# Attention's steps put in another order, a float64 decode of four operations, and 48 warm-up products more

## The chip, the cores and the metric

One Trainium2 chip, one of its cores. The metric is device time in microseconds (us) of one execution, from the first to the last instruction with what lies around them. The kernel before takes 933.77 us (median of 3 runs, 930.19 to 936.92). Engines: PE multiplies matrices, DVE and ACT work elementwise, POOL does a little elementwise work and the gathers, SP issues most of the transfers. Each engine runs its own instructions strictly in the order of the program and waits where the next one's input isn't there or its output tile isn't free.

## The reference

Three stages, one behind the other, on 2304 tokens (4 batches of 576) of width 512 (8 heads of 64):

- attention by landmarks: for every batch and head, 32 landmark queries and keys are means over 18 tokens; three softmax score matrices A (576x32), Bm (32x32), C (32x576); six Newton steps turn Bm into an approximate inverse Z; the result is A Z C v.
- a dense layer: `h = x @ w_in` (512 to 2048), `softplus(h) @ w_out` (2048 to 512).
- a mixture of experts: argmax over 8 gates picks one expert per token, `relu(x @ w1[e]) @ w2[e]`, scaled by two gate factors.

`w_in` and `w_out` arrive as float64 (the factors of 8 and of 1/sqrt make them so), q, k, v as float32. A float64 weight is read as two 32-bit words and turned into a float32 on the chip ("decode"); every float32 operand of the dense layers is then split into a high and a low fp32r part, and each product is made of three (high x high, high x low, low x high).

## The kernel before, in words

**Attention** works on 8 groups of four heads (group g: batch g // 2, heads 4 (g % 2) on). Its work is cut into named steps: K (load k and q of a group), V (load v), T (24 transposes of k and q on PE, evicted by ACT, L180 to L192), M (landmarks), A and C (scores and softmax, most of the DVE work), E (transposes of C's exponentials and the product with v), N (Bm and the Newton steps, for a batch), F (the last products, `ps_x`, evicted into `xo`, of which there are three, and stored to `xT_d` in DRAM, L363 to L387), W (one of 16 blocks of 128 columns of `w_in`: loaded, decoded, split into `whi`, `wlo`, L389), O (the same for the first block of `w_out`), X (the first 256 tokens' x, loaded back from DRAM and split, L414). `PLAN` (L38) lists these steps, and the place in that list is a step's priority. The order on each engine is then worked out by a planner with modelled costs: an instruction that is ready by its estimate goes ahead of one with a higher priority that isn't. So a step late in the list can run early if its tiles are free. In attention the order of the list is thus a wish; from the dense layer on (`with tc.manual_schedule()`, L848) each engine's order is that of the program text.

Loads of k, q and v have three tiles each (`ld`, L147), so K3 waits for K0's tiles. W, O and X have two tiles `raw` of their own in the same pool. Small matrix products of a constant tile `dense` with itself (`warm`, L161) are put ahead of real work on PE into the tile that the work will overwrite; they keep PE busy and compute nothing that is used: 18 at the start, one per tensor in T (at `h == 0`), and some in A, C, E and F.

**Decode** (L87): ACT takes the absolute value of the upper word (L93), DVE shifts it left by 3 and masks it (L94), puts the sign in (L96), puts three bits of the lower word in (L98), and multiplies by 0 where the magnitude is under a bound (L101, the guard). A yield stands after each DVE operation, so that the caller can spread them.

**Dense layer.** Chunks of 256 tokens. The first three chunks (`JOINT`) take turns over 8 pairs of blocks; 24 turns in all. Per turn i: 24 products of `gemm1`, softplus (ACT: abs L636, exp L637, +1 L638, ln L640; DVE: L641, then a turn later L647, L648; ACT copies the high part, L654; DVE the low part, L655), and 12 products of `gemm2` for turn i - 2. Beside these turns the 21 blocks of weights not yet there are decoded ("jobs", `weights()`, L580), one per turn: `units(n)` runs the next n pieces of the job list, `U` says how many at three places of a turn (behind L647 and L648 of turn i - 1 and `gemm1`; behind softplus; ahead of `gemm2`). The tiles `t`, `u`, `l`, `d` of softplus have one buffer each. The first three jobs are done ahead of the first turn (`units(15)`, five pieces each).

Pools opened later lie over memory of closed ones. Most wait tile by tile (`reuse_waits="tile"`); `gp` (L451), which lies lowest and holds among others the tiles `wg`, `tri_b`, `one_b`, doesn't: its instructions wait for whole pools below it. Before, that is `ld`, opened first (L147) and so lowest. The first instructions of the dense part are two loads of x, a load of a weight block, the two loads of `wg` on SP, and the casts to `tri_b` and `one_b` on DVE (L850 to L855).

The pieces of a job are, with the line of each operation:

```
piece 1: L93 (ACT), L94 (DVE)      piece 2: L96      piece 3: L98
piece 4: L101, next load           piece 5: L109 (ACT), L110 (DVE)
```

Of the kernel before, what the change touches and what calls it, by code (L numbers as in the profile page):

```python
# [10 lines left out]
F32 = DT.float32  # L11
# [24 lines left out]
HALF = S // 2  # L36
NB = 1
PLAN = """  # L38
M0 M1 K2 T0 V0 C0 A0 M2 T1 E0 A1 V1 C1 T2 K3 C2 M3 K4 K5 T3 E1 V2 K6 M4 T4 V3 W0 W1 C3 A2 N0 F0 T5 N1 A3 V4 A4 W2 E2
V5 M5 W3 E3 K7 M6 C4 C5 T6 C6 E4 A5 N2 M7 W4 V6 F1 V7 T7 N3 C7 E5 E6 A6 A7 E7 O0 F2 W5 W6 X0 F3 W7 W8 W9  # L40
"""
NWA = 10
JOINT = 3
# [1 line left out]
TAIL = 0, 2, 1, 0, 1, 1, 0, 0, 1, 0, 1, 0, 0, 0, 1, 1  # L45
NBASE = NTILE + NE // 2 + 1
LEAD = 1
U = 1, 2, 2
LAG = 2


# [32 lines left out]
CONST, COFF = const_table()  # L84


def decode_f64(nc, pool, src, shape, tag="dect", guard="vector", **kw):  # L87

    w = src.rearrange("p a (n two) -> p a n two", two=2)
    lo32, hi32 = w[:, :, :, 0], w[:, :, :, 1]  # L90
    t = pool.tile(shape, I32, tag=tag, name="dect", **kw)
    a = pool.tile(shape, F32, tag="deca", name="deca", **kw)
    nc.scalar.activation(a, hi32.bitcast(F32), AF.Abs)  # L93
    nc.vector.tensor_scalar(t, a.bitcast(I32), 3, 0x3FFFFFFF, ALU.logical_shift_left, ALU.bitwise_and)  # L94
    yield
    nc.vector.scalar_tensor_tensor(t, hi32, -0x40000000, t, ALU.bitwise_and, ALU.bitwise_or)  # L96
    yield
    nc.vector.scalar_tensor_tensor(t, lo32, 29, t, ALU.logical_shift_right, ALU.bitwise_or)  # L98
    yield
    if guard == "vector":  # L100
        nc.vector.scalar_tensor_tensor(a, a, 3.4332275390625e-05, t.bitcast(F32), ALU.is_ge, ALU.mult)  # L101
    else:
        nc.gpsimd.tensor_scalar(a, a, 3.4332275390625e-05, None, ALU.is_ge)
        nc.gpsimd.tensor_tensor(a, a, t.bitcast(F32), ALU.mult)
    yield a


# [11 lines left out]
def moe_nystrom_kernel(ctx: ExitStack, tc: tile.TileContext, q, k, v, w_in, w_out, w_gate, w_ogate, w1, w2,  # L119
# [24 lines left out]


    with ExitStack() as actx:
        ld = actx.enter_context(tc.tile_pool(name="a_ld", bufs=3))  # L147
        a1 = actx.enter_context(tc.tile_pool(name="a1", bufs=1))
        a2 = actx.enter_context(tc.tile_pool(name="a2", bufs=2))
        a3 = actx.enter_context(tc.tile_pool(name="a3", bufs=3))  # L150
        pt = actx.enter_context(tc.tile_pool(name="pt", bufs=2, space=PSUM))
        pss = actx.enter_context(tc.tile_pool(name="pss", bufs=2, space=PSUM))
        psm = actx.enter_context(tc.tile_pool(name="psm", bufs=1, space=PSUM))
# [7 lines left out]
        def warm(ps):  # L161

            nc.tensor.matmul(ps, dense[:, :128], dense, start=True, stop=True)
# [16 lines left out]
        def transposes(r, g):  # L180
            for nm in ("k", "q"):
                xt = a2.tile([128, 4, HALF], F32, tag=nm + "T", name=nm + "T", bufs=3)
                for h in range(4):
                    ps = pt.tile([128, 512], F32, tag="pt", name="ps_t")
                    if h == 0:
                        warm(ps)
                    for c in range(3):
                        nc.tensor.transpose(ps[:, c * TP:(c + 1) * TP], r[nm][:, h, c * 128:(c + 1) * 128],
                                            ident[:TP, :TP])
                    nc.scalar.activation(xt[:, h], ps[:, :HALF], AF.Copy)  # L190
                    yield
                r[nm + "T"] = xt  # L192
# [195 lines left out]

        def decode_w_in(i):  # L389
            n = FF // 16  # L390
            raw = ld.tile([128, 8 * n], I32, tag="raw", name="raw", bufs=2).rearrange("p (k f) -> p k f", k=4)
            nc.sync.dma_start(raw, w_in.bitcast(I32).rearrange("(k p) f -> p k f", p=128)[:, :, 2 * n * i:2 * n * (i + 1)])
            a = list(decode_f64(nc, a3, raw, [128, 4, n], bufs=2))[-1]
            split_hi_lo(nc, a, whi[0][:, :, i * n:(i + 1) * n], wlo[0][:, :, i * n:(i + 1) * n], nc.gpsimd)
# [8 lines left out]
            return [R[2 * b], R[2 * b + 1]]  # L403

        nc.scalar.preload_act_table_set("natural_log_exp_and_others")
        ps0 = psm.tile([128, 512], F32, tag="sm0", name="ps_0")
        for _ in range(18):
            warm(ps0)
        nc.sync.dma_start(cst[:, :128], consts[:, :128])
        nc.sync.dma_start(lmc, consts[:, CONST.shape[1] - 98:])  # L410
        load_qk(0)
        load_qk(1)
        nc.sync.dma_start(cst[:, 128:], consts[:, 128:CONST.shape[1] - 98])
        def prep_x0():  # L414
            xr = ld.tile([128, 4, CH], F32, tag="raw", name="x0r", bufs=2)
            nc.sync.dma_start(xr, xT_d[0].rearrange("(k p) n -> p k n", p=128)[:, :, :CH])
            split_hi_lo(nc, xr, x0[0], x0[1], nc.gpsimd)

        def prep_wo0():
            raw = ld.tile([128, 2 * DM], I32, tag="raw", name="raw", bufs=2)  # L420
            nc.sync.dma_start(raw, w_out.bitcast(I32)[:128, :])
            a = list(decode_f64(nc, a3, raw.unsqueeze(1), [128, 1, DM], bufs=2))[-1]
            split_hi_lo(nc, a[:, 0], wo0[0], wo0[1], nc.gpsimd)
# [128 lines left out]
    with ExitStack() as mctx:  # L552
# [295 lines left out]
        with tc.manual_schedule():  # L848
# [32 lines left out]
            for j in (1, 2):  # L881
                xs[j] = split_x(xr.pop(0))
                load_w(j)
            units(15)
            for i in range(len(order) + LAG):
                fast[0] = len(order) - np_ <= i - LAG + 1 < len(order)
                if i == len(order):
# [207 lines left out]
```

## Time and profile before

| | |
|---|---|
| median of 3 runs | 933.77 us (930.19 to 936.92) |
| the profiled execution | 929.7 us, its span 927.9 us |
| busy share of the span | PE 93%, PE weight loads 77%, DVE 73%, ACT 63%, POOL 23% |
| attention | until the first `gemm1` product at 159.0 us |
| turns with decode | to about 286 us |

The profile cuts the span into stretches; for each it gives the busy time of each engine, the clock that PE was granted (1.00 is full speed) and how busy the transfers were. The timeline lists instructions in order of time: start, duration, engine, line, and in brackets the idle time of the engine ahead of it with what ended it.

### The profile page before, as it was taken

What the parts mean: (1) busy time and instruction counts of PE and PEld (TensorE: products, weight loads), DVE (VectorE), ACT (ScalarE), POOL (GpSimd) and SP (SyncE); (2) the same over time, 40 slices, a digit from 0 to 9 for tenths busy, and PEclk for the clock granted to TensorE, in tenths of its full rate; (3) what the DMA queues carried; (4) which work ended last, traced back from release to release, by engine and by line L of the source; (5) the groups of instructions that cost most, each with busy time, mean ns of one, the idle gap of its engine ahead of it and who ended that gap; (6) DMA issues with size and microseconds to landing.
All of it is one profiled execution on the core that took longest, in us unless ns stands there. A gap on an engine that the chain in (4) does not pass through costs nothing.

```text
span 927.9 us, 15459 instructions
## 1 busy us (share of the span) xinstructions
PE 867.0 (93%) x5796; PEld 717.6 (77%) x5796; DVE 678.3 (73%) x1153; ACT 586.8 (63%) x958; POOL 212.7 (23%) x109
## 2 busy tenths in 40 slices
PE   7877897889999999999999999998999999999996
PEld 4444564777878899999899998886778888878885
DVE  1796975788886445565556454657899998899994
ACT  2465644666666555555555556464888988988883
POOL 0122200000000000000000000015566676766662
PEclk8899998899999999999999999999999999999998
DMA  9975345222210000100111000141116559531600
GB/s 234 227 207 166 99 146 172 91 91 69 91 46 23 24 1 24 33 15 23 46 47 46 1 24 1 46 183 46 35 46 246 188 169 362 202 129 35 222 31 32
DMA packets 49661, 90.93 MB, mean 98 GB/s; under 512 B 5487, under 2 KB 32239, under 8 KB 47536
## 3 DMA queue, kind: packets, MB, share of 16 engines
q1 hardware_dynamic: 41552, 74.43, 25.5%
q0 software_dynamic: 3680, 10.78, 3.6%
q10 hardware_dynamic: 4352, 4.72, 1.5%
q8 instruction: 46, 0.75, 0.3%
q14 instruction: 31, 0.25, 0.1%
HBM read 134.46 MB, written 15.48 MB: 162 GB/s over the span
## 4 chain that ended last, share of the span: by engine, by line
PE 54%; DVE 20%; DMA 9%; ACT 9%; issue 6%; SPq 1%; POOL 1%; ACTq 0%; DVEq 0%; POOLq 0%
PE ps_h L626 16%; PE acc L665 13%; PE ps_g L964 8%; PE ps_y L990 7%; DMA raw<-in_moe_w 3%; DMA raw<-in_moe_w_in 3%; DVE lo L486 3%; DVE dect L98 2%; DVE dect L96 2%; ACT hi L484 2%; DVE gl L655 2%; PE ps_lg L690 2%; ACT gh L654 2%; DVE l L648 1%; DVE d L647 1%
## 5 line engine op out<-in xcount | busy, mean ns | idle before, releaser
L486 DVE TENSOR_TENSOR lo<-raw,hi 128x1024 fp32r<-128x1024 f32 x129 | 223.4, 1758 | 14.5 <-ACT hi L484 14.2
L484 ACT ACTIVATE hi<-raw 128x1024 fp32r<-128x1024 f32 x176 | 177.2, 1063 | 12.1 <-DMA raw<-in_moe_w 11.1
L626 PE MATMUL ps_h<-xh,whi 128*128 128x256 f32 x512 | 148.1, 289 | 7.9 <-DVE d L647 6.1
L493 POOL DMA_INDIRECT xg<-x_d,gidx x23 | 37.8, 1645 | 497.3 <-ACT t L636 486.3
L626 PE MATMUL ps_h<-xl,whi 128*128 128x256 f32 x512 | 145.6, 284 | 0.3 <-DVE xl L110 0.3
L626 PE MATMUL ps_h<-xh,wlo 128*128 128x256 f32 x512 | 145.5, 284 | 0.0
L655 DVE TENSOR_TENSOR gl<-l,gh 128x512 fp32r<-128x512 f32 x72 | 49.8, 692 | 122.0 <-ACT gh L654 120.5
L486 POOL TENSOR_TENSOR lo<-raw,hi 128x1024 fp32r<-128x1024 f32 x47 | 118.4, 2522 | 38.8 <-ACT hi L484 38.7
L626 PEld LDWEIGHTS ps_h<-xh,whi 128*128 128x128 f32 x512 | 98.5, 192 | 13.5 <-DVE d L647 9.9
L626 PEld LDWEIGHTS ps_h<-xl,whi 128*128 128x128 f32 x512 | 98.7, 193 | 1.9 <-DVE xl L110 0.5
L626 PEld LDWEIGHTS ps_h<-xh,wlo 128*128 128x128 f32 x512 | 98.7, 193 | 0.0
L665 PE MATMUL acc<-woh,gh 128*128 128x512 f32 x240 | 96.0, 400 | 0.0
L665 PE MATMUL acc<-wol,gh 128*128 128x512 f32 x240 | 94.3, 393 | 0.0
L665 PE MATMUL acc<-woh,gl 128*128 128x512 f32 x240 | 94.0, 392 | 0.0
L636 ACT ACTIVATE t<-ps_h 128x512 f32<-128x512 f32 x72 | 42.6, 591 | 70.4 <-PE ps_h L626 49.2
L640 ACT ACTIVATE l<-t 128x512 f32<-128x512 f32 x72 | 45.5, 632 | 55.1 <-DVE gl L655 55.1
L990 PE MATMUL ps_y<-hi,hh 128*128 128x512 f32 x184 | 76.0, 413 | 0.3 <-ACT hh L982 0.2
L990 PE MATMUL ps_y<-hi,hlo 128*128 128x512 f32 x184 | 73.1, 397 | 1.7 <-DVE hlo L983 1.6
L964 PE MATMUL ps_g<-hi,x0l 128*128 128x512 f32 x184 | 73.7, 400 | 0.4
L990 PE MATMUL ps_y<-lo,hh 128*128 128x512 f32 x184 | 72.2, 392 | 0.0
L964 PE MATMUL ps_g<-lo,x0h 128*128 128x512 f32 x184 | 72.1, 392 | 0.0
L964 PE MATMUL ps_g<-hi,x0h 128*128 128x512 f32 x184 | 72.0, 392 | 0.0
(265 smaller groups left out, 1804.1 us busy)
## 6 DMA issues: line engine op xcount, KB each, us to landing
raw<-in_moe_w SPq DMA_DIRECT2D x88, 1024.0 KB
raw<-in_moe_w_in SPq DMA_DIRECT2D x16, 512.0 KB
raw<-in_moe_w_out SPq DMA_DIRECT2D x16, 512.0 KB
x_d<-x SPq DMA_DIRECT2D x9, 514.0 KB
k<-in_k SPq DMA_DIRECT2D x8, 576.0 KB
q<-in_q SPq DMA_DIRECT2D x8, 576.0 KB
v<-in_v SPq DMA_DIRECT2D x8, 576.0 KB
xT_d<-xo ACTq DMA_DIRECT2D x16, 288.0 KB
```

Of the source, the lines that this page charges most:

```text
L96: nc.vector.scalar_tensor_tensor(t, hi32, -0x40000000, t, ALU.bitwise_and, ALU.bitwise_or)
L98: nc.vector.scalar_tensor_tensor(t, lo32, 29, t, ALU.logical_shift_right, ALU.bitwise_or)
L484: nc.scalar.activation(w[0][:, us], raw[i][:, us], AF.Copy)
L486: eng.tensor_tensor(w[1][:, us], raw[i][:, us], w[0][:, us].bitcast(F32), ALU.subtract)
L493: nc.gpsimd.indirect_dma_start(out=xg, out_offset=None, in_=src, in_offset=bass.IndirectOffsetOnAxis(ap=gidx[:, s:s + 1], axis=0))
L626: nc.tensor.matmul(ps[:, i], a[:, kk], b_[:, kk], start=n == 0, stop=n == 11)
L636: nc.scalar.activation(t, h, AF.Abs)
L640: nc.scalar.activation(l, t, AF.Ln, bias=1.0)
L655: nc.vector.tensor_tensor(gl, l, gh.bitcast(F32), ALU.subtract)
L665: nc.tensor.matmul(acc[tt], a[:, i, ts_], b_[f], start=f == 0 and n == 0, stop=f == NFF - 1 and n == 2)
L964: nc.tensor.matmul(ps, a[:, kk], b_[:, kk], start=n == 0, stop=n == 11)
L990: nc.tensor.matmul(y, a[:, kk], b_[:, kk], start=half == 0 and n == 0, stop=half == 1 and n == 11)
```

## The change

Three things at once. **Decode**: L93 scales by 2^-112 while it takes the absolute value, so that the mask and the guard are left out; the last operation writes the result. A job has four pieces instead of five: `units(15)` becomes `units(12)` and `U` goes from 1, 2, 2 to 1, 1, 2. **Attention**: another `PLAN`, in which blocks of `w_in` come late (W0 to W7 in the last third, W8 and W9 at the end); the blocks, O and X take their tiles from those of k, q and v in turn instead of from two of their own; `ld` is opened last, so that `a1` (with `dense`) and `a2` lie lowest; K1's load stands in `PLAN`, the constants but `lmc` come in one load behind K0's. **Warm-up products**: none of the 18 at the start; four per tensor in T instead of one.

```diff
 PLAN = """
-M0 M1 K2 T0 V0 C0 A0 M2 T1 E0 A1 V1 C1 T2 K3 C2 M3 K4 K5 T3 E1 V2 K6 M4 T4 V3 W0 W1 C3 A2 N0 F0 T5 N1 A3 V4 A4 W2 E2
-V5 M5 W3 E3 K7 M6 C4 C5 T6 C6 E4 A5 N2 M7 W4 V6 F1 V7 T7 N3 C7 E5 E6 A6 A7 E7 O0 F2 W5 W6 X0 F3 W7 W8 W9
+K1 T0 M0 M1 A0 C0 T1 K2 M2 C1 K3 V0 A1 K4 V1 T2 E0 C2 E1 T3 M3 N0 V2 K5 K6 V3 T4 A2 C3 A3 F0 V4 E2 M4 A4 M5 T5 K7 E3
+N1 X0 V5 M6 C4 T6 C5 C6 E4 M7 V6 V7 N2 A5 E5 W0 F1 N3 W1 W2 E6 W3 T7 A6 W4 O0 C7 A7 W5 F2 W6 E7 W7 F3 W8 W9
 """
-U = 1, 2, 2
+U = 1, 1, 2
...
-    nc.scalar.activation(a, hi32.bitcast(F32), AF.Abs)
-    nc.vector.tensor_scalar(t, a.bitcast(I32), 3, 0x3FFFFFFF, ALU.logical_shift_left, ALU.bitwise_and)
+    nc.scalar.activation(a, hi32.bitcast(F32), AF.Abs, scale=2.0 ** -112)
+    nc.vector.tensor_scalar(t, a.bitcast(I32), 3, None, ALU.logical_shift_left)
     yield
-    nc.vector.scalar_tensor_tensor(t, hi32, -0x40000000, t, ALU.bitwise_and, ALU.bitwise_or)
+    nc.vector.scalar_tensor_tensor(t, hi32, -0x80000000, t, ALU.bitwise_and, ALU.bitwise_or)
     yield
-    nc.vector.scalar_tensor_tensor(t, lo32, 29, t, ALU.logical_shift_right, ALU.bitwise_or)
-    yield
-    if guard == "vector":
-        nc.vector.scalar_tensor_tensor(a, a, 3.4332275390625e-05, t.bitcast(F32), ALU.is_ge, ALU.mult)
-    else:
...
+    nc.vector.scalar_tensor_tensor(a.bitcast(I32), lo32, 29, t, ALU.logical_shift_right, ALU.bitwise_or)
     yield a
...
-        ld = actx.enter_context(tc.tile_pool(name="a_ld", bufs=3))
         a1 = actx.enter_context(tc.tile_pool(name="a1", bufs=1))
         a2 = actx.enter_context(tc.tile_pool(name="a2", bufs=2))
         a3 = actx.enter_context(tc.tile_pool(name="a3", bufs=3))
+        ld = actx.enter_context(tc.tile_pool(name="a_ld", bufs=3))
...
                     ps = pt.tile([128, 512], F32, tag="pt", name="ps_t")
-                    if h == 0:
-                        warm(ps)
+                    warm(ps)
...
         def decode_w_in(i):
-            raw = ld.tile([128, 8 * n], I32, tag="raw", name="raw", bufs=2).rearrange("p (k f) -> p k f", k=4)
+            raw = ld.tile([128, NC6 * 4 * D], I32, tag="kqv"[i % 3], name="raw")
+            raw = raw[:, :8 * n].rearrange("p (k f) -> p k f", k=4)
...
-        ps0 = psm.tile([128, 512], F32, tag="sm0", name="ps_0")
-        for _ in range(18):
-            warm(ps0)
-        nc.sync.dma_start(cst[:, :128], consts[:, :128])
         nc.sync.dma_start(lmc, consts[:, CONST.shape[1] - 98:])
         load_qk(0)
-        load_qk(1)
-        nc.sync.dma_start(cst[:, 128:], consts[:, 128:CONST.shape[1] - 98])
+        nc.sync.dma_start(cst, consts[:, :CONST.shape[1] - 98])
         def prep_x0():
-            xr = ld.tile([128, 4, CH], F32, tag="raw", name="x0r", bufs=2)
+            xr = ld.tile([128, 4, CH], F32, tag="k", name="x0r")
...
-            raw = ld.tile([128, 2 * DM], I32, tag="raw", name="raw", bufs=2)
+            raw = ld.tile([128, 2 * DM], I32, tag="q", name="raw")
...
-            units(15)
+            units(12)
```

## Rows read from the trace of the kernel before

**Rows 1.** Busy us per stretch: PE, PEld, DVE, ACT, POOL, PEclk, DMA share, GB/s.
```profile
9.00:60.00 51.00, 41.00 (x471) 26.22 (x464) 31.73 (x79) 23.21 (x57) 5.20 (x4) 0.80 0.91 225
60.00:75.00 15.00, 11.17 (x165) 7.35 (x164) 15.00 (x36) 10.34 (x27) 4.89 (x3) 1.00 0.73 206
100.00:145.00 45.00, 42.54 (x636) 28.83 (x633) 39.57 (x121) 23.50 (x55) 3.82 (x3) 1.00 0.34 100
145.00:159.00 14.00, 8.44 (x39) 3.27 (x38) 5.51 (x9) 7.12 (x12) 0.00 (x0) 0.84 0.81 261
178.00:286.00 108.00, 98.69 (x604) 84.45 (x604) 94.45 (x152) 68.29 (x118) 0.00 (x0) 1.00 0.23 71
```

**Rows 2.** The guard, L101, alone: DVE busy per stretch, with its count.
```profile
0.00:80.00 80.00, 6.54 (x8) 0.87 0.85 217
80.00:145.00 65.00, 2.03 (x3) 0.97 0.40 118
```

**Rows 3.** Waits from 0 to 160 us: total us, times, longest.
```profile
ACT deca L93 <- DMA raw<-in_moe_w_in: 10.0, 6, 3.8
ACT xo L383 <- DMA xT_d<-xo: 6.0, 4, 2.5
```

**Rows 4.** Timeline of PE, two warm-up products that follow each other.
```profile
137.70 0.38 PE L163 MATMUL ps_x<-dense 128*128 128x512 bf16 x1
137.91 0.38 PE L163 MATMUL ps_et<-dense 128*128 128x512 bf16 x1
```

**Rows 5.** Timeline of DVE, one turn with decode.
```profile
209.31 0.69 DVE L110 TENSOR_TENSOR wol<-deca,woh 128x512 fp32r<-128x512 f32 x1 [0.62 <-ACT woh L109]
...
210.38 0.70 DVE L96 SCALAR_TENSOR_TENSOR dect<-raw,dect 128x512 int32<-128x512 int32 x1
211.11 0.69 DVE L98 SCALAR_TENSOR_TENSOR dect<-raw,dect 128x512 int32<-128x512 int32 x1
...
212.44 0.69 DVE L648 TENSOR_TENSOR l<-l,d 128x512 f32<-128x512 f32 x1
213.04 0.68 DVE L101 SCALAR_TENSOR_TENSOR deca<-deca,dect 128x512 f32<-128x512 f32 x1
213.83 0.69 DVE L655 TENSOR_TENSOR gl<-l,gh 128x512 fp32r<-128x512 f32 x1
214.44 0.68 DVE L641 SCALAR_TENSOR_TENSOR u<-u,t 128x512 f32<-128x512 f32 x1
```

**Rows 6.** Timeline of ACT, the same turn.
```profile
208.67 0.61 ACT L109 ACTIVATE woh<-deca 128x512 fp32r<-128x512 f32 x1
209.19 0.65 ACT L93 ACTIVATE deca<-raw 128x512 f32<-128x512 f32 x1
209.74 0.58 ACT L636 ACTIVATE t<-ps_h 128x512 f32<-128x512 f32 x1
...
213.16 0.63 ACT L654 ACTIVATE gh<-l 128x512 fp32r<-128x512 f32 x1
...
215.09 0.62 ACT L109 ACTIVATE whi<-deca 128x512 fp32r<-128x512 f32 x1
```

**Rows 7.** Timeline of ACT, a turn after the last job.
```profile
297.64 0.60 ACT L636 ACTIVATE t<-ps_h 128x512 f32<-128x512 f32 x1 [1.78 <-PE ps_h L626]
298.27 0.63 ACT L637 ACTIVATE t<-t 128x512 f32<-128x512 f32 x1
298.94 0.63 ACT L638 ACTIVATE u<-t 128x512 f32<-128x512 f32 x1
299.48 0.61 ACT L654 ACTIVATE gh<-l 128x512 fp32r<-128x512 f32 x1
```

**Rows 8.** Timeline of ACT, the third of the jobs ahead of the turns.
```profile
167.20 0.63 ACT L109 ACTIVATE woh<-deca 128x512 fp32r<-128x512 f32 x1 [2.70 <-DVE deca L101]
```

**Rows 9.** Timeline of DVE, the first cast of the dense part.
```profile
144.02 0.23 DVE L854 CAST tri_b<-cst 128x128 bf16<-128x128 f32 x1 [0.26 <-PE ps_cv L355]
```

**Rows 10.** Timeline of PE, attention's last warm-up product.
```profile
156.16 0.59 PE L163 MATMUL ps_x<-dense 128*128 128x512 bf16 x1 [2.13 <-ACT xo L383]
```

More of the change, by code (lines that the diff above doesn't have):

```diff
@@ L84, with decode_f64 @@
 CONST, COFF = const_table()
-def decode_f64(nc, pool, src, shape, tag="dect", guard="vector", **kw):
+def decode_f64(nc, pool, src, shape, tag="dect", **kw):
     w = src.rearrange("p a (n two) -> p a n two", two=2)
@@ L92, in decode_f64 @@
     a = pool.tile(shape, F32, tag="deca", name="deca", **kw)
-    nc.scalar.activation(a, hi32.bitcast(F32), AF.Abs)
-    nc.vector.tensor_scalar(t, a.bitcast(I32), 3, 0x3FFFFFFF, ALU.logical_shift_left, ALU.bitwise_and)
+    nc.scalar.activation(a, hi32.bitcast(F32), AF.Abs, scale=2.0 ** -112)
+    nc.vector.tensor_scalar(t, a.bitcast(I32), 3, None, ALU.logical_shift_left)
     yield
-    nc.vector.scalar_tensor_tensor(t, hi32, -0x40000000, t, ALU.bitwise_and, ALU.bitwise_or)
+    nc.vector.scalar_tensor_tensor(t, hi32, -0x80000000, t, ALU.bitwise_and, ALU.bitwise_or)
     yield
-    nc.vector.scalar_tensor_tensor(t, lo32, 29, t, ALU.logical_shift_right, ALU.bitwise_or)
-    yield
-    if guard == "vector":
-        nc.vector.scalar_tensor_tensor(a, a, 3.4332275390625e-05, t.bitcast(F32), ALU.is_ge, ALU.mult)
-    else:
-        nc.gpsimd.tensor_scalar(a, a, 3.4332275390625e-05, None, ALU.is_ge)
-        nc.gpsimd.tensor_tensor(a, a, t.bitcast(F32), ALU.mult)
+    nc.vector.scalar_tensor_tensor(a.bitcast(I32), lo32, 29, t, ALU.logical_shift_right, ALU.bitwise_or)
     yield a
```

## The prediction

> **What bounds the kernel now.** I read the busy share by stretch first, since the three stages have different limits, then the waits of attention, then the timelines of DVE and ACT for one turn of the dense layer. Nothing behind the turns with decode is touched: the experts, the later chunks and their tiles stay as they are. So two stretches decide.
>
> In attention no engine is full for long [rows 1]. From 9 to 60 us PE is busy 41 of 51 us at a granted clock of 0.80 (a mean of its two levels, 1.2 and 2.4 GHz) and the transfers run at 0.91; from 60 to 75 us DVE never rests; from 100 to 145 us PE does 42.5 of 45 and DVE 39.6; from 145 to 159 us all of them wait, mostly for the stores of `xo`. ACT loses 10.0 us in six waits for blocks of `w_in` and 6.0 us in four for those stores [rows 3]. Attention is thus PE's in its second half, and a mixture in its first.
>
> In the turns with decode DVE (94 of 108 us) and PE (99) both look nearly full [rows 1], yet neither sets the time. Take one turn from high copy to high copy, 208.67 to 215.09: 6.42 us [rows 6]. Follow who waits for whom [rows 5, 6]: L109 on ACT, 0.64 later L110 on DVE, then L94 and at 210.38 L96, 0.73 later L98, 1.33 later (past L647) L648, 0.72 later L654 on ACT, 0.67 later L655 on DVE, and 1.26 later (past ACT's L640, which needs the tile `l` that L655 has read) the next L109. These steps sum to 6.42. L101 at 213.04 runs while ACT makes L654: it isn't in that ring.
>
> **The change, part by part.** First the turns, where the order can be followed by hand. The new pieces are: L93, L94; L96; L98; L109 with L110. By i = 2 the job list stands so that one turn holds, on DVE: L647, L648, L94, L655, L641, L96, L98, L110; on ACT: L93, L636, L637, L638, L654, L640, L109. The new ring goes the other way round through ACT: L109 to L93 0.52, L93 to L636 0.55 [rows 6], L636 to L637 0.63, L637 to L638 0.67, L638 to L654 0.54 [rows 7], L654 to L655 0.67, L655 to L641 0.61, L641 to L96 0.61 (as L655 to L641, no dependence), L96 to L98 0.73 [rows 5], L98 to L109 0.73 (as L648 to L654, with the hop). Sum 6.26. The guard's 0.69 us are gone, but they weren't in the old ring, and the new order puts L96 and L98 between softplus and the next high copy, with L93 ahead of the next L636. That is 0.16 less per turn; 108 us hold 17 turns: **-2.7**. Bounds: -12 (17 x 0.69, everything the guard took) to +2 (hops 0.1 dearer than read). I take the ring. PE's own work per turn, 98.7/108 x 6.42 = 5.9, still hides.
>
> Ahead of the turns, three jobs follow one another through ACT and DVE; the third's L109 waited 2.70 us for decode [rows 8]. Two such waits lose 0.69 each: -1.4. Against it stands `gp`. Before, it lies over `ld` and its first cast went at 144.02, just behind the last reader of v, `ps_cv` [rows 9], while F3 was still waiting for stores. With `ld` opened last, `gp` lies over `a1` and `a2`; the last reader there is the warm-up product ahead of F3's last `ps_x`, at 156.16 [rows 10]. DVE then has the casts, four L110 for x at 0.61, and a decode of 1.8 (0.46 + 0.73 + 0.61, from rows 5) still to do, some 5 us, of which 2.8 fit ahead of the first `gemm1` at 159.0: +2.2. SP has the second and third weight block queued behind the `wg` loads that wait likewise; they are needed 3 us later than the first, so at most another 3 us. Net **+1**, bounds -1.4 to +5.
>
> Attention, against its 159.0 us:
> - 48 more warm-up products. Two in a row start 0.21 apart [rows 4]: 10.1 us of PE if none falls in a gap, 0 if all do. PE is busy 80% of 9 to 60 us and 95% of 100 to 145; T also waits for ACT's evictions. I take **+6**.
> - 11 guards, 8.6 us of DVE [rows 2]. They count only where DVE never rests: **-3**, bounds -8.6 to 0.
> - No block of `w_in` can be loaded early: W0 needs K6's tile, W2 that of V5, W8 that of V7, which is free only behind E7. ACT's 10 us of waits at those loads [rows 3] fall away in the first half. PE and DVE had other work or waited for K and V beside them: **-5**, bounds -10 to 0.
> - The same blocks now come in the last third. 8 of 11 decodes lay before 80 us [rows 2]; at 1.8 us each that is 14.4 us of DVE put where it rests 5.4 of 45 us and is rid of three guards (2.0): 7 us too much, up to 14 if its rests can't be used. It frees 20 us of DVE in the first half, where PE has 3.8 idle us beside a full DVE [rows 1]: **+2**, bounds -4 to +14. If those late loads land late, ACT waits in order, and softmax and evictions are queued behind them.
> - F2 stands ahead of E7, no longer next to F3, so the three `xo` tiles meet four stores, not eight: **-3** of the 6.0 [rows 3], bounds -6 to 0.
> - The start: 18 products that ran while nothing was loaded, and the constants behind K0 instead of split; T0 stands first and DVE's softmax may start earlier. The clock of 0.80 would give back at most 8 us of 41 if it rose to full. I take 0, bounds -8 to +2.
>
> L93 with a scale and L94 with one operation are taken at their old length: L637 runs with a scale in 0.63 us against L638's 0.63 with none [rows 7]. Attention: 6 - 3 - 5 + 2 - 3 = **-3**. All: -3 + 1 - 2.7 = -4.7. The profiled execution took 929.7, so 925.0 by it; the median of the runs is 4.1 above that, and the forecast against it is **929**.
>
> **The rivals.**
> *The turns follow DVE's load.* If the ring has slack that I don't see, a turn loses all of the guard's 0.69 us: -11.7 instead of -2.7, 920. For it: DVE is busy 87% of that stretch [rows 1], PE's floor of 5.9 leaves room. Against: L101 starts beside L654 and DVE still idles 0.62 ahead of L110 [rows 5]. The Trainium skill says the same in "VectorE: DVE Perf Modes", section "Rules for kernel authors": for chained operations, keep down their number. By that rule the time would be 920; the trace doesn't bear it out for an operation off the ring. Chance 0.14.
>
> *Attention keeps the gain of its first half.* The loads of k, q, v have the transfers for themselves, ACT's waits go in full (-10 for -5), the start gives 3, and the late blocks fit into rests (-2 for +2): -12 more, 917. For: from 9 to 60 us DVE rests 19 of 51 us and PE 10 [rows 1], with next to nothing but those loads to wait for. Against: PE's second half is full before any product is added. Chance 0.20.
>
> *The late blocks lengthen the end.* DVE has no rest from about 100 us to F3, W5 to W9 are decoded on DVE and ACT ahead of what the dense part needs first, and the first `gemm1` starts after 170 instead of 159.0. Price: 14 instead of 2, and +4 at the start of the turns: 945. It decides if DVE is over 95% busy from 100 us to the end of attention. For: 7 us too much by the sum above. Against: W8 and W9 are needed only in later turns, and 14 us behind 145 us stand half empty. Chance 0.22.
>
> *All added warm-up products lie on PE's path*, and the front gives nothing (+4 and +5): 938. Chance 0.06. *The decode costs as before*, if an absolute value with a scale or a shift without a mask ran slower: 11 and 21 decodes, 0.2 us each, would be under 4 us in the ring; it stays inside the forecast.
>
> **How the numbers follow.** A change of 1%, 9.3 us, is about what can be told from none. The forecast has 0.38, its own range 922 to 939. Faster by over 1% (under 924.4): the first two rivals, 0.34. Within: forecast and warm-up case, 0.44. Slower (over 943.1): 0.22. The range leaves out the outer halves of the second and third rivals: 913 to 947.
>
> **What would show it.** Turn: L109 to L109 at 6.2 to 6.3 us, L98 straight ahead of L109, no idle of DVE but behind L109 and L654. `tri_b` right behind the last warm-up product. Few waits of ACT for `w_in` before 60 us, and the fourth softmax (A3) before 75 us. DVE over 90% busy in the last 45 us of attention, PE too; the first `gemm1` at 152 to 162. Wrong: a turn under 6.0 or over 6.5, attention's end outside 148 to 168, or any difference behind the turns.

## The result, and the profile after

The changed kernel takes **919.01 us** (median of four runs, 917.9 to 920.92) against 934.41 us for the kernel before on the same chip in the same job (four runs, 930.19 to 936.92): a ratio of 0.9862, interval 0.9834 to 0.9889. The forecast was 929, its own case 922 to 939, the whole range 913 to 947. The time lies in the range, but not in the forecast's own case; it is near rival 2's 917. The profiled execution took 920.92, with a span of 919.1 against 927.9.

PE's granted clock over the span comes first, from the page of the changed kernel (40 slices of 23 us, in tenths of full speed; 9 is 90% or more).

```profile
PEclk9999997799999999999999999999999999999998
```

The first six slices, 138 us, now have 90% or more. The two at 7 are where attention ends and the turns start. Next the busy time by stretch of the changed kernel, with the columns of [rows 1].

```profile
9.00:60.00 51.00, 48.31 (x628) 32.66 (x629) 26.95 (x77) 25.88 (x66) 0.00 (x0) 1.00 0.85 195
60.00:75.00 15.00, 14.97 (x213) 9.16 (x213) 8.80 (x30) 6.96 (x15) 0.00 (x0) 1.00 0.64 169
100.00:145.00 45.00, 39.36 (x467) 23.86 (x465) 37.25 (x91) 27.58 (x58) 9.24 (x7) 0.97 0.55 167
145.00:159.00 14.00, 12.46 (x75) 10.45 (x76) 9.26 (x19) 6.41 (x12) 2.65 (x2) 0.72 0.79 246
```

From 9 to 60 us PE is busy 48.31 us, not 41.00, at 1.00 instead of 0.80. DVE has fallen from 31.73 to 26.95 there, and from 15.00 to 8.80 in the next stretch. What the clock does there is seen best from 20 to 30 us, first in the kernel before, then in the changed one (with its next 10 us).

```profile
20.00:30.00 10.00, 10.00 (x97) 5.42 (x96) 3.97 (x20) 2.96 (x8) 0.00 (x0) 0.58 1.10 258
```
```profile
20.00:30.00 10.00, 9.28 (x145) 5.81 (x140) 8.06 (x26) 5.65 (x15) 0.00 (x0) 1.00 1.11 246
30.00:40.00 10.00, 10.00 (x125) 7.13 (x118) 9.13 (x29) 4.58 (x12) 0.00 (x0) 1.00 0.76 176
```

Before, PE never rested in that stretch, at a granted 0.58, and got through 97 products; the changed kernel does 145 in 9.28 busy us at 1.00, about 10 of them warm-up products (2 before). A busy share alone doesn't show such a loss.

From 100 to 145 us PE and DVE are at 87% and 83%: neither is full, though eight decodes fall into that stretch. The blocks are counted by the last operation of a decode, L101, alone (DVE busy and count), to be set against [rows 2]; DVE is the column behind the length.

```profile
0.00:80.00 80.00, 0.00 (x0) 1.00 0.79 185
80.00:145.00 65.00, 7.67 (x10) 0.98 0.55 166
```

The view of waits from 0 to 160 us of the changed kernel (total, times, longest) answers to [rows 3].

```profile
ACT deca L96 <- DMA raw<-in_moe_w_in: 4.2, 2, 3.0
ACT deca L96 <- DMA raw<-in_moe_w_out: 2.5, 1, 2.5
```

ACT's wait for blocks of `w_in` fell from 10.0 to 4.2 us, and the 6.0 us at the stores of `xo` are gone. The 2.5 us for a block of `w_out` lie behind attention; the kernel before had one such wait, of 1.4 us.

The front can be followed by four marks: the start of each softmax (A0 to A3, the transpose of `asm`), the first and second `wbd` (F0, F1), the first `gemm1`, and the first softplus of the dense part (L628; L636 before).

| us | A0 | A1 | A2 | A3 | F0 | F1 | first `gemm1` | first softplus | turn |
|---|---|---|---|---|---|---|---|---|---|
| before | 30.8 | 41.4 | 59.5 | 84.4 | 76.4 | 119.8 | 159.0 | 167.7 | 6.42 |
| after | 21.4 | 31.6 | 42.7 | 57.9 | 61.1 | 110.4 | 149.7 | 164.4 | 6.22 |

The gain is 9.4 us at A0, 26.5 at A3, 15.3 at F0, 9.4 at F1 and 9.3 at the first `gemm1`. Attention thus wins in its first half and gives part of it back in the last third. Then 6.0 of the 9.3 are lost at once: from the first `gemm1` to the first softplus it is 14.7 us, before 8.7. This is the timeline of the changed kernel there, PE's products first, then DVE, ACT and the DMA queue of SP, and last two rows of ACT in the kernel before.

```profile
147.43 0.61 PE L160 MATMUL ps_x<-dense 128*128 128x512 bf16 x1
149.67 0.58 PE L618 MATMUL ps_h<-x0h,whi 128*128 128x256 f32 x1 [0.37 <-ACT xo L379]
```
```profile
147.21 0.69 DVE L101 SCALAR_TENSOR_TENSOR deca<-raw,dect 128x512 int32<-128x512 int32 x1
148.08 0.23 DVE L846 CAST tri_b<-cst 128x128 bf16<-128x128 f32 x1 [0.18 <-PE ps_x L160]
...
150.73 0.69 DVE L107 TENSOR_TENSOR xl<-xr,xh 128x512 fp32r<-128x512 f32 x1 [0.27 <-ACT xh L106]
```
```profile
147.94 0.63 ACT L106 ACTIVATE whi<-deca 128x512 fp32r<-128x512 f32 x1 [2.31 <-DVE deca L101]
...
152.17 0.68 ACT L96 ACTIVATE deca<-raw 128x512 f32<-128x512 f32 x1
154.90 0.63 ACT L106 ACTIVATE woh<-deca 128x512 fp32r<-128x512 f32 x1 [2.05 <-DVE deca L101]
158.07 0.69 ACT L96 ACTIVATE deca<-raw 128x512 f32<-128x512 f32 x1 [2.54 <-DMA raw<-in_moe_w_out]
...
164.41 0.58 ACT L628 ACTIVATE t<-ps_h 128x512 f32<-128x512 f32 x1
```
```profile
150.48 0.37 SPq L845 DMA_DIRECT2D wg<-in_moe_w_gate  x1
...
151.56 30.79 SPq L567 DMA_DIRECT2D raw<-in_moe_w_out  x8
```
```profile
149.12 0.67 ACT L93 ACTIVATE deca<-raw 128x512 f32<-128x512 f32 x1
...
159.40 0.63 ACT L109 ACTIVATE woh<-deca 128x512 fp32r<-128x512 f32 x1 [0.44 <-ACT xo L383]
```

The 6.0 us come apart into three pieces. Before, ACT began the first weight block at 149.12, long ahead of the first `gemm1` at 159.0, between evictions of `xo`, and made its high copy 0.4 us behind that product. Now ACT is late with it: it makes W9's high copy at 147.94 after 2.31 us of waiting for DVE, then the four of x and two evictions of `xo`, and only then, at 152.17, the first L96; the high copy at 154.90 is 5.2 us behind the first `gemm1`: +4.8. The second weight block lands late and stops ACT 2.54 us at 158.07: +2.5. The two jobs behind the first are shorter than their 3.9 us before: -1.4.

`tri_b` goes 0.04 us behind the end of the last warm-up product (147.43 + 0.61), as predicted, but it delays nothing that can be seen: the first L96 is 2.50 us behind the first `gemm1` here, and 2.50 in run 8, where the casts stand elsewhere. The second weight block is issued behind the `wg` loads, yet these hold it by 0.1 us at most: its tile is that of the second chunk's x, whose split (L107) ends at 151.42, and it goes at 151.56. It then takes 6.5 us to land.

Last, one turn of the changed kernel, ACT from high copy to high copy and DVE beside it. It answers to [rows 5, 6].

```profile
181.99 0.63 ACT L106 ACTIVATE woh<-deca 128x512 fp32r<-128x512 f32 x1 [1.30 <-DVE deca L101]
182.52 0.67 ACT L96 ACTIVATE deca<-raw 128x512 f32<-128x512 f32 x1
183.10 0.57 ACT L628 ACTIVATE t<-ps_h 128x512 f32<-128x512 f32 x1
183.70 0.63 ACT L629 ACTIVATE t<-t 128x512 f32<-128x512 f32 x1
184.37 0.64 ACT L630 ACTIVATE u<-t 128x512 f32<-128x512 f32 x1
184.91 0.61 ACT L646 ACTIVATE gh<-l 128x512 fp32r<-128x512 f32 x1
...
188.21 0.63 ACT L106 ACTIVATE woh<-deca 128x512 fp32r<-128x512 f32 x1 [1.30 <-DVE deca L101]
```
```profile
185.55 0.69 DVE L647 TENSOR_TENSOR gl<-l,gh 128x512 fp32r<-128x512 f32 x1 [0.55 <-ACT gh L646]
186.16 0.68 DVE L633 SCALAR_TENSOR_TENSOR u<-u,t 128x512 f32<-128x512 f32 x1
186.76 0.69 DVE L99 SCALAR_TENSOR_TENSOR dect<-raw,dect 128x512 int32<-128x512 int32 x1
187.48 0.69 DVE L101 SCALAR_TENSOR_TENSOR deca<-raw,dect 128x512 int32<-128x512 int32 x1
188.88 0.69 DVE L107 TENSOR_TENSOR wol<-deca,woh 128x512 fp32r<-128x512 f32 x1 [0.70 <-ACT woh L106]
```

Start to start the ring has 0.53, 0.58, 0.60, 0.67, 0.54, 0.64, 0.61, 0.60, 0.72 and 0.73: 6.22 us, down ACT to L646, over to L647 on DVE, and back with L101 to L106. DVE has two pauses, ahead of L647 and of L107, and so isn't the bound.

Where the profiled execution's time went, each term as the difference of the same instruction's start in the two traces (in the turns the logarithm, L632, L640 before; at the end the last `ps_g` product of the experts):

| stretch | forecast | measured |
|---|---|---|
| attention, to the first `gemm1` | -3 | -9.3 |
| first `gemm1` to first softplus (turn 0) | +1 | +6.0 |
| turn 0 to turn 2 | 0 | +0.9 |
| 18 turns, 2 to 20 | -2.7 | -3.5 |
| the next chunk's x, by turn 24 | 0 | -1.4 |
| behind the turns | 0 | -1.2 |
| sum | -4.7 | -8.5 |

By the first softplus the two misses nearly cancel: -3.3 for a forecast -2. The last 2.6 us come behind the turns with decode, for which the forecast had nothing; "any difference behind the turns" was one of its signs of being wrong. What makes them was not found.

### The profile page after: what moved, and what is told of

Read it like the earlier page. It is cut to its first block, busy times and chain, and to the rows that moved or that the text cites. A ratio compares the mean times of both kernels' runs of the same rounds, so it can differ in the third digit from the quotient of the medians.

```text
span 919.1 us, 15441 instructions
## 1 busy us (share of the span) xinstructions
PE 863.8 (94%) x5826; PEld 717.5 (78%) x5826; DVE 660.8 (72%) x1121; ACT 589.2 (64%) x958; POOL 209.6 (23%) x109
## 4 chain that ended last, share of the span: by engine, by line
PE 68%; DVE 13%; ACT 10%; issue 4%; DMA 4%; POOL 0%; SPq 0%; POOLq 0%; ACTq 0%; DVEq 0%
PE ps_h L618 16%; PE acc L657 14%; PE ps_g L956 12%; PE ps_y L982 11%; DVE dect L99 2%; DVE deca L101 2%; PE ps_hT L970 2%; PE ps_lg L682 2%; ACT t L629 2%; ACT u L630 2%; ACT deca L96 2%; ACT gh L646 1%; DVE u L633 1%; PE ps_t L184 1%; PE ps_t L160 1%
## 5 line engine op out<-in xcount | busy, mean ns | idle before, releaser
L478 DVE TENSOR_TENSOR lo<-raw,hi 128x1024 fp32r<-128x1024 f32 x129 | 228.7, 1799 | 8.8 <-ACT hi L476 8.6
L647 DVE TENSOR_TENSOR gl<-l,gh 128x512 fp32r<-128x512 f32 x72 | 49.9, 692 | 129.0 <-ACT gh L646 129.0
L478 POOL TENSOR_TENSOR lo<-raw,hi 128x1024 fp32r<-128x1024 f32 x47 | 115.9, 2468 | 35.3 <-ACT hi L476 35.2
L628 ACT ACTIVATE t<-ps_h 128x512 f32<-128x512 f32 x72 | 42.6, 592 | 69.6 <-PE ps_h L618 50.0
L632 ACT ACTIVATE l<-t 128x512 f32<-128x512 f32 x72 | 45.5, 632 | 55.1 <-DVE gl L647 55.1
```

The lines of the kernel that those rows point to most:

```text
L478: eng.tensor_tensor(w[1][:, us], raw[i][:, us], w[0][:, us].bitcast(F32), ALU.subtract)
L628: nc.scalar.activation(t, h, AF.Abs)
L632: nc.scalar.activation(l, t, AF.Ln, bias=1.0)
L647: nc.vector.tensor_tensor(gl, l, gh.bitcast(F32), ALU.subtract)
```

## The experiments

Two theories of attention's gain stood against each other. The **clock theory**: the added warm-up products keep PE's clock at 2.4 GHz while K and V are still coming. The **list theory**: the blocks of `w_in`, coming late, no longer stop ACT, and PE is fed. Beside them stood the question which part the decode plays, and whether its turn is a ring or DVE's load. Where no other baseline is named, a ratio is against the kernel before in the same job.

One caution holds for all runs that touch attention: the planner orders it anew for each kernel. Set side by side, the traces show run 2 in the changed kernel's order up to 91 us and run 4 up to 73, but run 3 only up to 22 us; of the old order run 1 leaves at 33 us and runs 5 and 6 at 22. Run 9 keeps the order of run 4 until ACT comes to the first early block. So runs 1, 3, 5 and 6 each try a piece of the change together with another order. Runs 7, 8, 11 and 12 have the changed kernel's order in all of attention, and their first `gemm1` still lies anywhere from 147.0 to 148.9 us, against 149.7: a difference of 2 or 3 us between two traces is no finding.

**1. The new decode alone, in the kernel before.**

```diff
-    nc.scalar.activation(a, hi32.bitcast(F32), AF.Abs)
+    nc.scalar.activation(a, hi32.bitcast(F32), AF.Abs, scale=2.0 ** -112)
...
-U = 1, 2, 2
+U = 1, 1, 2
-            units(15)
+            units(12)
```

> The kernel before with the new decode alone (no mask, no guard, four pieces per job, U = 1, 1, 2; attention's list, tiles and warm-up products as before). By the ring: a turn falls from 6.42 to 6.2 us, 17 turns give 3 us, the jobs ahead of the turns 1.4, attention's first gemm1 stays within 3 us of 159.0: a ratio of 0.993 to 0.998 to before. If the decode is what made the change fast: 0.985 to 0.988, with the first gemm1 near 150.

Ratio 1.0031 (1.0001 to 1.0061), 936.13 us. The turn is 6.22 us, so the decode does its work there, and the kernel is no faster: its attention runs otherwise, with the first `gemm1` at 174.3, PE's clock at 0.75 from 9 to 60 us and 9.7 us of ACT waits for `w_in`. (The profiled execution, 941.2, is the slowest of its ten.) So one operation less per block brings nothing by itself here. The shorter decode changed the order of attention, as said above; that this order is what costs is only argued.

**2. The old decode in the changed kernel.** Its diff is the first one reversed.

> The changed kernel with the old decode (mask, guard, five pieces, U = 1, 2, 2). If attention's order and its warm-up products made the gain: the first gemm1 at 149 to 154, turns of 6.42 us, ratio to before 0.989 to 0.994. If the decode made it: the first gemm1 at 157 or later and a ratio of 0.998 or more.

Ratio 0.9953 (0.9927 to 0.9979), 928.03 us, just outside the 0.989 to 0.994 that was expected. First softmax 20.6, A3 57.1, F0 60.3, first `gemm1` 152.4, clock 1.00: attention's gain is there without the new decode. The turn is 6.42 again, and the first `ps_g` of the experts is 7.2 us later than in the changed kernel: 2.7 to the first `gemm1`, 0.5 to the first softplus, 2.5 in the turns to turn 20, 1.5 by turn 24. So attention's gain is the work of the other two parts, and the decode saves about 9 us (928.0 to 919.0, in two jobs) on top of it.

**3. One warm-up product per tensor in the changed kernel**, as before.

```diff
-                    warm(ps)
+                    if h == 0:
+                        warm(ps)
```

> The changed kernel with one warm-up product per tensor in T, as before, instead of four (48 fewer; none at the start either). Theory of the clock: the granted clock from 9 to 60 us falls from 1.00 to 0.85 or less, and the first gemm1 moves from 149.7 to 155 or later: ratio to before 0.992 or more. Rival, the products lie on PE's path: clock stays, PE loses up to 10 us of work, the first gemm1 comes at 146 or earlier: ratio 0.983 or less.

Ratio 0.9966 (0.994 to 0.9992), 927.39 us: 48 products less, with the order that the planner makes without them, cost some 8 us. The busy time by stretch of this kernel:

```profile
20.00:30.00 10.00, 8.36 (x103) 4.64 (x96) 6.16 (x14) 3.15 (x8) 0.00 (x0) 0.90 1.11 236
30.00:40.00 10.00, 9.98 (x95) 5.49 (x93) 5.46 (x25) 3.46 (x11) 0.00 (x0) 0.59 0.59 141
```

The changed kernel has PE busy 9.28 us in the first of these and 10.00 in the second, both at 1.00. Here PE falls to 8.36 busy us, and the next 10 us are granted 0.59: PE doesn't rest there, and does 95 products instead of 125. From 9 to 60 us the clock is 0.90, not the 0.85 or less that was expected. A1 starts at 39.0 (31.6 in the changed kernel) and the first `gemm1` at 156.2. These 6.5 us shrink to 2.3 at the first softplus and are 5.9 at the end of the span, so the path from attention to the time isn't a straight one. The sign of the forecast's +6 for these products was wrong in this list.

**4. Own tiles for the blocks in the changed kernel**: two of their own, as before the change, with the new list.

```diff
-            raw = ld.tile([128, NC6 * 4 * D], I32, tag="kqv"[i % 3], name="raw")
-            raw = raw[:, :8 * n].rearrange("p (k f) -> p k f", k=4)
+            raw = ld.tile([128, 8 * n], I32, tag="raw", name="raw", bufs=2).rearrange("p (k f) -> p k f", k=4)
...
```

> The changed kernel with two tiles of their own for the blocks of w_in, O and X, as before, so that blocks can be loaded from the start. Theory of the late blocks: ACT waits for w_in before 66 us come back (8 us or more), the clock stays at 1.00, the first gemm1 moves to 154 or later: ratio to before 0.990 or more. Theory of the clock alone: the first gemm1 within 2 us of 149.7, ratio 0.984 to 0.988.

Ratio 0.989 (0.9836 to 0.9944), 922.57 us; first `gemm1` 152.0. ACT waits 14.1 us for `w_in`, in nine waits, yet the longest is 2.5 and A0 to A3 are as in the changed kernel: the list puts the blocks late whichever tiles they have, and none is decoded in the first 60 us. So the tile, the forecast's reason for late blocks, isn't the cause; the place in the list may be. Run 9 tests it.

**5. Four warm-up products per tensor in the kernel before.**

```diff
-                    if h == 0:
-                        warm(ps)
+                    warm(ps)
```

> The kernel before with four warm-up products per tensor in T instead of one (48 more), and nothing else of the change. Theory of the clock: the granted clock from 9 to 60 us rises from 0.80 to 0.95 or more, the first gemm1 comes at 152 to 156 instead of 159.0, runs scatter less: ratio to before 0.992 to 0.997. Rival, the new list is what lets PE run on, and the products only add work on PE's path: first gemm1 at 160 or later, ratio 1.000 or more.

Ratio 1.0066 (1.004 to 1.0092), 935.8 us, slower. The granted clock from 9 to 60 us rises to 0.90, the first `gemm1` stays at 158.9, and ACT waits 8.8 us for `w_in`. Alone, the products cost about 6 us, the size of the forecast's term, and the higher clock shortens nothing. Where the 6 us lie isn't shown: the profiled execution, at 931.11 the fastest of the ten, has its first `gemm1` where the kernel before has it.

**6. New decode and four warm-up products in the kernel before**: both of the diffs above.

> The kernel before with the new decode and four warm-up products per tensor: everything of the change but the list of steps, the shared tiles, the pool order and the start. If those add nothing: first gemm1 at 150 to 154, turns of 6.22, ratio to before 0.984 to 0.989, as the whole change. If the list carries its own part (early blocks of w_in stop ACT, 8 us or more before 66 us): first gemm1 at 156 or later, ratio 0.992 or more.

Ratio 1.0054 (1.0029 to 1.0079), 933.32 us. ACT waits 17.7 us for `w_in`, and the first `gemm1` is at 166.1. New decode and warm-up products without the rest (the list, the shared tiles, the order of the pools, the start) give nothing: the rest carries a part of its own.

**7. L101 in the guard's old place, in the changed kernel.**

```diff
-U = 1, 1, 2
+U = 1, 2, 1
...
-                u = ((0, 0, 3), (0, 2, 3))[i] if i < 2 else U
+                u = ((0, 0, 3), (0, 1, 2))[i] if i < 2 else U
```

> The changed kernel with U = 1, 2, 1 and the second turn's 0, 1, 2, so that L101 (the last operation of a decode) stands beside ACT's high copy, where the guard stood. By the ring: 6.42 less 0.73 for one operation that leaves it, 5.7 us per turn instead of 6.22; 16 turns give 8 us less: ratio to the changed kernel 0.991, to before 0.976 to 0.981. If something else (PE, the order of pieces) holds the turn at 6 us or more: ratio to before 0.984 or more.

Ratio 0.9771 (0.9751 to 0.9791), 908.27 us. One turn of DVE, the order ahead of the next low copy:

```profile
185.52 0.69 DVE L107 TENSOR_TENSOR wol<-deca,woh 128x512 fp32r<-128x512 f32 x1 [0.62 <-ACT woh L106]
186.13 0.42 DVE L97 TENSOR_SCALAR dect<-deca 128x512 int32<-128x512 int32 x1
186.59 0.69 DVE L99 SCALAR_TENSOR_TENSOR dect<-raw,dect 128x512 int32<-128x512 int32 x1
187.20 0.68 DVE L639 SCALAR_TENSOR_TENSOR d<-ps_h,u 128x512 f32<-128x512 f32 x1
187.91 0.69 DVE L640 TENSOR_TENSOR l<-l,d 128x512 f32<-128x512 f32 x1
188.52 0.68 DVE L101 SCALAR_TENSOR_TENSOR deca<-raw,dect 128x512 int32<-128x512 int32 x1
189.30 0.69 DVE L647 TENSOR_TENSOR gl<-l,gh 128x512 fp32r<-128x512 f32 x1
...
191.22 0.69 DVE L107 TENSOR_TENSOR wol<-deca,woh 128x512 fp32r<-128x512 f32 x1 [0.62 <-ACT woh L106]
```

The turn is 5.69 or 5.70 us. DVE has the same eight operations as in the changed kernel, in another order. L101 runs while ACT makes L646 and is off the ring, which now goes by L106, L107, L97, L99, L639, L640, L646, L647, L632: the old ring of [rows 5, 6] less one operation of 0.73. The ring theory gave 5.7 for it; a turn bound by DVE's load would not have moved. PE is now close behind: it is busy 82.00 of the 82 us from 178 to 260 us, and a turn without decode takes 5.62 in this trace as in those of the two kernels. So the ring has some 0.07 us per turn left to give.

**8. `gp`'s loads and casts behind the three jobs, in the changed kernel.** What is moved is the two `wg` loads, `tri_b`, `one_b`, `osum` and `sgn`.

```diff
-            for nm, src in ((0, w_gate), (1, w_ogate)):
-                nc.sync.dma_start(wg[:, :, nm * NE:(nm + 1) * NE], src.rearrange("(k p) e -> p k e", p=128))
-            nc.vector.tensor_copy(tri_b, cc("tri"))
...
             units(12)
+            for nm, src in ((0, w_gate), (1, w_ogate)):
+                nc.sync.dma_start(wg[:, :, nm * NE:(nm + 1) * NE], src.rearrange("(k p) e -> p k e", p=128))
+            nc.vector.tensor_copy(tri_b, cc("tri"))
...
```

> The changed kernel with the first instructions of gp (the two loads of wg, the casts) moved behind the first three weight loads and the jobs ahead of the turns. If gp's wait is what delays the start: ACT's wait of 2.5 us for the second weight block goes, the first abs of softplus comes 11 to 13 us behind the first gemm1 instead of 14.7: ratio to the changed kernel 0.997 to 0.998, to before 0.982 to 0.985. If that load is late for another reason (its tile is free only behind the split of x): the wait stays, no difference.

Ratio 0.9873 (0.9852 to 0.9894), 917.5 us. The wait of 2.54 us is gone, and from the first `gemm1` to the first softplus it is 12.1 us instead of 14.7. But `gp`'s place isn't shown to be the reason. The second weight block is issued 1.8 us behind the first `gemm1`, in the changed kernel 1.9, and in run 7, which has `gp` where the changed kernel has it, the same wait is 0.41 us and the stretch 12.6. How long that load takes to land differs from trace to trace. The time, some 1.5 us under the changed kernel's across two jobs, can't be told from no change.

**9. Early blocks, in the kernel of run 4**: the same tiles, W0 to W4 moved to about where the old list had them.

```diff
-... K5 K6 V3 T4 A2 C3 A3 F0 V4 E2 M4 A4 M5 T5 ...
+... K5 K6 V3 T4 W0 W1 A2 C3 A3 F0 V4 E2 M4 A4 W2 M5 W3 T5 ...
```

> The kernel of e4 (the change with two tiles of their own for the blocks) with W0 to W4 put in the list where the kernel before has them (behind T4, A4, M5, M7), nothing else. Theory of the late blocks: their decode enters the first 60 us again, ACT waits there for w_in, A3 starts at 65 us or later instead of 57.7, the first gemm1 comes at 156 or later instead of 152.0: ratio to before 0.993 or more. Rival, the front is faster since T and A of the first group stand first: A3 before 61 us, first gemm1 within 2 us of 152.0, ratio 0.986 to 0.991.

Ratio 0.9976 (0.9951 to 1.0002), 930.25 us, against 0.989 of run 4. The busy time from 20 to 30 us, and the first block's L95 on ACT (the line is one lower in this kernel):

```profile
20.00:30.00 10.00, 2.92 (x63) 2.02 (x63) 3.32 (x6) 1.53 (x5) 0.00 (x0) 0.76 1.10 276
```
```profile
28.86 0.66 ACT L95 ACTIVATE deca<-raw 128x512 f32<-128x512 f32 x1 [8.40 <-DMA raw<-in_moe_w_in]
```

The waits of the same kernel from 20 to 31 us (total, times, longest) have the other end of it:

```profile
ACT deca L95 <- DMA raw<-in_moe_w_in: 8.4, 1, 8.4
...
PE ps_t L159 <- ACT lm L206: 7.1, 1, 7.1
```

This is the chain by itself: ACT comes to the decode of a block whose load shares the transfers with K and V (1.10 of their time), waits 8.40 us, and PE, which waits for an eviction queued behind it on ACT, has 2.92 busy us in ten. The clock is 0.76 there and 0.73 in the next ten. A0 is at 20.8, as early as in the changed kernel, but A1 starts at 42.2, not 31.3 as in run 4, and the first `gemm1` at 158.8, not 152.0. Four warm-up products per tensor are in this kernel, and they don't save it.

**10. Late blocks and four warm-up products in the kernel before**, with its order of tensors, pools and decode.

```diff
-... T4 V3 W0 W1 C3 A2 ... A4 W2 E2 V5 M5 W3 E3 ... M7 W4 V6 F1 V7 T7 N3 C7 E5 E6 A6 A7 E7 O0 F2 W5 W6 X0 F3 W7 W8 W9
+... T4 V3 C3 A2 ... A4 E2 V5 M5 E3 K7 X0 ... M7 V6 W0 F1 V7 W1 W2 T7 N3 W3 C7 E5 E6 W4 A6 O0 A7 W5 E7 F2 W6 W7 F3 W8 W9
...
-            raw = ld.tile([128, 8 * n], I32, tag="raw", name="raw", bufs=2).rearrange("p (k f) -> p k f", k=4)
+            raw = ld.tile([128, NC6 * 4 * D], I32, tag="kqv"[i % 3], name="raw")
```

> The kernel of e5 (before with four warm-up products per tensor) with the blocks, O and X late in the list and in the tiles of k, q and v, as in the change; old decode, old order of the other steps, old pool order, old start. Theory of the late blocks with the warm-up products: no decode in the first 60 us, clock 0.95 or more, A3 before 70 us instead of 84, first gemm1 at 155 or earlier: ratio to before 0.990 to 0.997. Rival, the other steps' order carries it: first gemm1 at 158 or later, ratio 1.000 or more.

Ratio 1.013 (1.0083 to 1.0177), 945.51 us: slower, and at rival 3's 945. But the place is another. No block is done before 100 us, the clock from 9 to 60 us is 0.90 (0.95 or more was expected), and A3 comes at 75.0: 9.4 us of the 26.5 that the changed kernel gains there, so the rest belongs to what run 10 leaves out, the other steps' order and the start among it. F1 at 110.6 is as good as the changed kernel's 110.4, and the first `gemm1` still at 159.6. Then it takes 25.5 us to the first softplus. Queue of SP, SP's own wait (total, times, longest) and DVE:

```profile
164.75 2.93 SPq L605 DMA_DIRECT2D xr<-xT_d  x6
```
```profile
SPq L605 <- DVE dect L97: 28.7, 1, 28.7
```
```profile
163.02 1.66 DVE L97 SCALAR_TENSOR_TENSOR dect<-raw,dect 128x512 int32<-128x512 int32 x1
164.78 0.69 DVE L100 SCALAR_TENSOR_TENSOR deca<-deca,dect 128x512 f32<-128x512 f32 x1
165.39 0.22 DVE L853 CAST tri_b<-cst 128x128 bf16<-128x128 f32 x1
```

With `ld` opened first, as before the change, the tiles of the next stage lie over it. The last block's L97 is the last reader of a tile in `ld` and ends at 164.68; the loads of x go at 164.75. In the changed kernel, with `ld` opened last, the same six loads were issued from 126.87 to 143.47 us, ahead of the last block's L101, which reads its tile last (147.21). Late blocks thus need the new order of the pools: read from these two traces, since no run changed the order of the pools alone.

**11. Runs 7 and 8 together.**

> The change with both mends: U = 1, 2, 1 (turns of 5.69 us) and gp's first instructions behind the loads and jobs. If both are paid in the same coin: 908.3 of e7 less 1 to 2 us, ratio to before 0.974 to 0.977. If gp's casts, now ahead of the first turns, delay these: no better than e7.

Ratio 0.9722 (0.968 to 0.9764), 907.65 us, no different from run 7's within the intervals. First `gemm1` 148.3, first softplus 160.6 (run 7: 147.0 and 159.6): moving `gp` gave nothing.

**12. Run 11, with the identity's 64 KB loaded first** and the other constants behind K0.

```diff
+        nc.sync.dma_start(cst[:, :128], consts[:, :128])
         nc.sync.dma_start(lmc, consts[:, CONST.shape[1] - 98:])
         load_qk(0)
-        nc.sync.dma_start(cst, consts[:, :CONST.shape[1] - 98])
+        nc.sync.dma_start(cst[:, 128:], consts[:, 128:CONST.shape[1] - 98])
```

> The kernel of e11 with the identity loaded first (64 KB), the other constants behind K0 as before, since PE waits 6.5 us for the one load of constants ahead of the first transposes. If that wait sets the start: the first softmax (A0) 1.5 us earlier than 20.4 to 21.4, and the same at the first gemm1: ratio to before 0.972 to 0.975. If K1, which waits in the same queue, or DVE is next: no difference from e11.

Ratio 0.9691 (0.965 to 0.9732), 905.3 us, the lowest measured, though not told apart from run 11. Ahead of the first transposes PE waits 3.9 us, for K0, instead of 7.0 for the constants, and A0 starts at 18.3 instead of 21.7. A2 is still 3.4 us earlier (39.6), but A3 comes at 58.0 against 58.2: the gain of the start is lost again between these two, and what takes it isn't shown. Runs 7, 11 and 12 beat both kernels.

## Why the prediction was wrong

**The step that failed is attention's sum, "6 - 3 - 5 + 2 - 3 = -3"**, measured -9.3; and in it the last term, "The start: ... I take 0, bounds -8 to +2", and the first, "I take +6". A0 alone came 9.4 us earlier, beyond the start's bound. Run 9 shows why that gain lasts: with the same early A0 but early blocks, ACT stops for a load, A1 is 10.9 us later than in run 4, and attention ends where the kernel before ends it.

Rival 2 (0.20) had the direction: late blocks free ACT, and attention keeps a gain. Its own sum for attention, -15 (12 more than -3), was about as far off as the forecast's, and ACT's waits did not go in full. That the time lies near its 917 is in part luck: in the traces 6.0 us are lost again at the start of the turns, and 4 to 7 us of the difference of the medians are not in the traces at all.

*Start and clock, forecast 0.* The granted clock went from 0.80 to 1.00 between 9 and 60 us, and PE had 48.3 busy us there for 41.0. It was taken as a by-product that nothing else depended on, while "The clock of 0.80 would give back at most 8 us of 41 if it rose to full" stood beside it as a bound. How much of the 9.3 is the clock's isn't separated. All runs of the kernel before show how clock and time go together. Over 56 of them (in three jobs), 17 with a mean granted clock of 0.975 or more have a median of 928.7 us, and 14 at 0.968 or less 935.6; a straight line through the 56 gives 5.8 us per 0.01. The changed kernel's four runs lie at 0.980 to 0.984, where the kernel before had a mean of 0.972. By that line 0.010 of clock goes with about 6 of the 13 us that the ratio stands for. The line is a correlation: a stretch in which PE is stalled shows a low clock too. It is no price either: run 5 has a mean clock of 0.978, for which the line gives 928, and took 935.8.

*Warm-up products, forecast +6.* In the old list they cost that (run 5, +0.0066, 6 us). In the new list they save 8 us (run 3). Both runs also have another order, so the products alone aren't priced. They seem to be worth something only where PE is otherwise fed; the forecast priced them as PE time alone.

*ACT's waits, forecast -5 within -10 to 0.* They fell by 5.8 (10.0 to 4.2). But they have a price that the waits don't show: run 9 puts them back, and the first `gemm1` comes 6.8 us later than in run 4, because PE empties behind ACT and the clock falls with it. Neither theory alone accounts for it. Runs 3 and 9 each take away one of the two conditions and lose most of the gain (run 3 with another order besides); runs 5, 6 and 10 give the kernel before one to three pieces of the change, and its time doesn't fall.

*Late blocks, forecast +2.* They probably cost: the gain is 15.3 us at F0 and 9.4 at F1, though other steps were moved there too. But DVE is 83% busy from 100 to 145 us, not over 90%, and rival 3's full DVE didn't come. Its price did in run 10, by another mechanism.

*Stores of `xo`, forecast -3 of 6.0.* All 6.0 us of those waits are gone; what that gave isn't separated. *Guards, -3:* run 2 gives 2.7 at the first `gemm1`, which fits, but equal attentions differ by as much.

**The start of the turns, forecast +1 within -1.4 to +5**, measured +6.0, failed too, and not by size alone. Its -1.4 for the shorter jobs is right. The casts behind the last warm-up product cost nothing that can be seen, and `wg` holds SP's queue by 0.1 us. What the sum missed is ACT: it has to finish the last block, W9, and x's four high copies before it can start the first weight block, at 152.17: +4.8. The other +2.5 is a late load; why it is late is open, and run 7 has 0.41 in its place.

**The turns, forecast 6.26 us**, measured 6.22, were right, with all ten hops within 0.03 of their forecasts. Run 7 shows that they are a ring. Rival 1, that the guard's 0.69 would go in full, falls: the turn lost 0.20. Between the old and the new decode in the same list (run 2) one operation less gave 0.20 us per turn, and in run 7 the same number of operations in another order 0.53. The rule of the Trainium skill that rival 1 was set beside ("VectorE: DVE Perf Modes", section "Rules for kernel authors": keep down the number of chained operations) thus holds here only in part. One reading was wrong without harm: PE's own work per turn is not 5.9 but 5.62 at most, the length of a turn without decode.

**Left open.** The profiled executions differ by 8.8 us, the medians by 13 to 15. The one of before lay at the low end of its runs (clock 0.975), the one of after at the high end of its own; the line above would give 1.8 us for the first. The rest isn't assigned. Nor is it shown which entry of the list brings A0 forward by 9 us: T0 and A0 come first and the 18 products at the start are gone, and the runs don't part these two. That the constants are one load isn't it: run 12 splits them again, and A0 is earlier still. Why the new decode alone makes the old front longer (run 1) was not found.

## What to carry to other kernels

Follow who waits for whom around one turn, and price an operation by whether it is on that ring: taking one off DVE gave 0.20 us, moving another one into its gap 0.53. Where a stage lives on arriving loads, look first for the load that an in-order engine stops for, and ask which engine idles behind it and what its clock does then; in this kernel fillers came with a gain only once that stop was gone. And before a pool's place or a load's time is changed, ask which tile's last reader the next stage waits for: work moved late pays there.

## What the runs showed of the hardware that was not expected

- The spread of one kernel's runs goes with its mean granted clock: the kernel before ran 925.4 to 938.2 us over 56 runs with a mean clock of 0.981 to 0.963, correlation -0.84, while the changed kernel kept to 917.9 to 920.9 and run 7 to 907.9 to 908.6, at 0.980 to 0.985.
- A busy PE can be a slow one: from 20 to 30 us the kernel before had PE busy all 10 us at a granted 0.58, with 97 products; the changed kernel did 145 in 9.28 busy us at 1.00.
- More filler can make a kernel faster: 48 products that compute nothing were worth some 8 us of 927 in run 3, and cost 6 of 930 in run 5, in each case together with the order that the planner made of them.
